# Softmax sums by another transfer queue, and weight copies off GpSimd

## The chip, the cores and the metric

The kernel runs on one core of a Trainium2 chip. The core has TensorE (matrix products), VectorE, ScalarE, GpSimd and SyncE (SP), each with an instruction queue of its own, and 16 engines for transfers. Time is that of the device for one execution, in microseconds (us); lower is better. In the rows, PE is TensorE's products, PEld its weight loads, DVE is VectorE, ACT ScalarE, POOL GpSimd, and SPq the queue of SP that issues transfers.

## What is computed

An attention over a window with sinks, and two feed-forward layers behind it. Shapes: 2 batches, 8 heads, 768 positions, head width 64; 4 sinks, window 128; 1536 tokens, model width 512, inner width 2048.

```python
scores = q @ k.T / 8                      # kept: the 4 sinks, and the last 128 positions up to the row
a = exp(scores - max); a = a / (sum(a) + 1e-9)
x = a @ v                                 # heads side by side: 1536 x 512
h = x @ w_in                              # first layer: a rational function
g = (a0 + a1*h + a2*h**2 + a3*h**3) / (1 + abs(b0)*abs(h) + abs(b1)*h**2 + 1e-6)
x = g @ w_out
h = x @ moe2_w_in                         # second layer: h * sigmoid(1.702 h)
out = (h * sigmoid(1.702*h)) @ moe2_w_out
```

The weights arrive as 64-bit floats and are turned into 32-bit ones on the chip.

## The kernel before

**Tiling.** The 1536 tokens are three blocks T of 512 (TB). The attention of a block works on pairs of heads, four pairs for each block, so there are twelve rounds. The feed-forward layers take the 2048 inner columns in 16 slices f of 128; a unit is a block with half of the slices, and UNITS gives their order, so that a weight slice serves several blocks before it is dropped. Each product of two 32-bit matrices is three TensorE products of a high and a low part (wh with xh, wh with xl, wl with xh).

**A weight slice** (decode, L629): SP loads it to wraw; ScalarE takes an absolute value (dy), VectorE clamps and shifts and joins (dy, dt); then `hi(WH, ...)` at L641 copies dt to the high part of wi or wo, on one of the engines that WH names, and VectorE subtracts that for the low part. There are 64 slices, and 64 copies of that kind.

**A round of the attention.** TensorE multiplies q and k; VectorE masks and finds the maximum (m, nm); ScalarE exponentiates (a) and sums (sm). sums (L978) adds 1e-9, takes the reciprocal (rs), has TensorE transpose the eight columns to eight rows, and copies them to rt (ScalarE or VectorE). One transfer writes rt to DRAM (rd); two transfers read it back to rb, each spreading four rows over 64 partitions (the two heads). Meanwhile TensorE transposes a, ScalarE or VectorE copies that to th and sT, and values (L1031) multiplies with v. VectorE multiplies that with rb, ScalarE rounds to xh, VectorE makes xl: the input of the first layer.

**The first layer's function** (el_a, L725). ScalarE makes y = |b0 h| and z from the square, and GpSimd issues a transfer that adds y to z in place (add, L544). ScalarE's logarithm and exponential then make the reciprocal r (el_b).

**The order.** Nothing is issued in the order of the program text. A planner (play, L292) simulates the five engines with a price for each operation and a due time: the longest path to the end plus BIAS of its class (at0 to at2: the attention of a block; wi00, wo01 and so on: the slices of layer and half; m0 to m7: the units). HEAD spaces the rounds of a block in that due time. An engine that becomes free takes its own most urgent ready operation, and, where it has none, one of another engine that has a form for it, if `spares` allows it:

```python
return max(free[p], now) + q + o.alts[p][0] > now + o.alts[e][0] + THETA   # L393
```

The first engine named in "act/dve/pool" is the owner p, the others may take over (e). What the planner wrote down is then the fixed order of each queue. Where TensorE has nothing ready in the first part, it gets filler products on zeros (L869). The transfers are planned with L234 to L237. A queue issues in order: an instruction that waits holds what stands behind it.

Of the kernel before, what the change touches and what calls it, by code (L numbers as in the profile page):

```python
# [6 lines left out]
F32R = mybir.dt.float32r  # L7
# [7 lines left out]
B, H, S, D = 2, 8, 768, 64  # L15
# [30 lines left out]
PSUM_TAGS, ANY_ORDER = ("h", "acc", "att"), ("att", "m")  # L46

GH2, GL2 = "act", "dve"
WH, WL, XH, S2, ST = "act/dve/pool", "dve", "act", "pool/dve", "act/dve"
TH, PE_OUT = "act/dve", "act/dve"  # L50

BIAS = {
# [4 lines left out]
}  # L57
HEAD = (5.81, 0.28, 18.6, 1.92)
THETA = -1.79

WARM, FILL, FILL_AHEAD = 20, 6000, 0.1

# [11 lines left out]
ADD_FIX, ADD_LAT = 0.9, 1.6  # L74
# [70 lines left out]
def overlap(a, b):  # L145
    return all(x[0] < y[1] and y[0] < x[1] for x, y in zip(a, b))


class Program:
# [56 lines left out]
    def op(self, eng, meth, alloc=(), alts=(), given=False, calls=(), cost=0.0, **kw):  # L206


        o = Op()
        o.i, o.eng, o.own = len(self.ops), eng, eng  # L210
        o.cat = self.cat
        o.table = 2 if kw.get("func") == AF.Sigmoid else 1 if kw.get("func") in (AF.Exp, AF.Ln) else 0
        views = [(k, v) for c in calls or [kw] for k, v in c.items() if isinstance(v, View)]

        def runner(eng, meth, kw):
            def run():
                a = {k: v.real() if isinstance(v, View) else v for k, v in kw.items()}
                e = getattr(self.nc, eng)
                if meth in ("matmul", "memset"):
                    return getattr(e, meth)(a.pop("out"), **a)  # L220
                return getattr(e, meth)(**a)  # L221
            return run
        o.lat = LAT
        o.nbytes = o.columns = 0
        if calls:
            runs = [runner(eng, meth, c) for c in calls]
            o.alts = {eng: (cost, lambda: [f() for f in runs][-1])}
            o.cost, o.lat = cost, PE_LAT
            o.columns = sum(c["rhs"].n * 4 * (c["lhsT"].box[0][1] - c["lhsT"].box[0][0]) / P if "rhs" in c else 2 * P for c in calls)
        elif meth == "dma_start":  # L230
            v = views[0][1]
            o.nbytes = (v.box[0][1] - v.box[0][0]) * v.n * 4
            o.cost, o.lat = 0.45 if v.box[0][1] - v.box[0][0] == P else 0.62, DMA_LAT
            if eng == "gpsimd":  # L234
                o.nbytes *= 2
                o.cost, o.lat = ADD_FIX, ADD_LAT + 0.6 * (kw["out"].dtype == F32R)
            o.alts = {eng: (o.cost, runner(eng, meth, kw))}  # L237
        else:
            self.columns = 0
            o.alts = {e: (self.price(e, m_, k_), runner(e, m_, k_)) for e, m_, k_ in [(eng, meth, kw)] + list(alts)}  # L240
            o.cost = min(c for c, _ in o.alts.values())
            o.columns = self.columns
            if eng == "tensor":
                o.lat = PE_LAT
        if given:
            o.alts, o.cost, o.lat, o.nbytes = {eng: (1e-6, lambda: None)}, 1e-6, given * 1.25 - 0.75, 0
        pre = {}
        for k, v in views:
            w = k in ("out", "accum_out")
            for q, box, wr in v.t.acc:  # L250
                if (w or wr) and overlap(box, v.box):
                    pre[q.i] = q
            if not v.t.acc:
                assert w, (v.t.name, k)
        o.allocs = [v.t for k, v in views if not v.t.acc] + [v.t for v in alloc if not v.t.acc]
        o.allocs = list(dict.fromkeys(o.allocs))
        o.begun = []
        for t in o.allocs:
            t.first = o
            t.acc.append((o, ((0, 0),), False))  # L260
        for t in dict.fromkeys([v.t for _, v in views] + [v.t for v in alloc]):
            if t not in o.allocs and not any(v.t is t for _, v in views):
                t.acc.append((o, ((0, 0),), False))
            if t.first is not o and t.first.i not in pre and (t.first.i, 0) not in pre:
                t.first.begun.append(o)
                pre[t.first.i, 0] = None
        for k, v in views:
            v.t.acc.append((o, v.box, k in ("out", "accum_out")))
        o.tiles = list(dict.fromkeys([v.t for _, v in views] + [v.t for v in alloc]))
        o.banks = [t for t in o.tiles if t.tag in PSUM_TAGS]  # L270
        o.preds = len(pre)
        o.succ = []
        o.next = []
        for q in pre.values():
            if q is not None:
                q.succ.append(o)
        o.ready = 0.0
        self.ops.append(o)
        return o
# [12 lines left out]
    def play(self):  # L292
# [92 lines left out]
        def spares(o, e):  # L385
# [3 lines left out]
            for t, i in own[p]:  # L389
                if t >= -o.prio:  # L390
                    break
                q += ops[i].alts[p][0]
            return max(free[p], now) + q + o.alts[p][0] > now + o.alts[e][0] + THETA  # L393

# [112 lines left out]
def emit(tc, qT, kX, vL, w_in, w_out, ca, cb, nw, out):  # L507
    nc = tc.nc
    R = Program(nc, tc)
# [12 lines left out]
    def hi(eng, o, i):  # L522
        l = eng.split("/")
        return one_of([form(e, o, i) for e in l])
# [3 lines left out]
    def tt(eng, op, out, in0, in1):  # L528
        return one_of([(NAMES[e], "tensor_tensor", dict(out=out, in0=in0, in1=in1, op=op)) for e in eng.split("/")])
# [322 lines left out]
    def build_banded():  # L852
        with (
# [23 lines left out]
            def attention(T, xs, alone):  # L877
# [49 lines left out]
                def pst(kind):  # L927
                    if alone and kind == "s":
                        return R.tile(ps, [P, 512], F32, tag="acc", name="pss", bufs=4)
                    if alone and kind == "v":  # L930
                        return R.tile(ps, [P, 512], F32, tag="h", name="psv", bufs=H_BUFS)
                    return R.tile(ps, [P, 512], F32, tag="att", name="psa", bufs=8 - 4 - H_BUFS)
# [45 lines left out]
                def sums(h):  # L978

                    sm = st.pop(("sm", h))  # L980
                    assert nq == 4
                    rs = R.tile(ap, [P, 8], F32, tag="rs", name="rs", bufs=2)
                    R.op("vector", "tensor_scalar", out=rs, in0=sm, scalar1=EPS_SM, scalar2=None, op0=ALU.add)
                    R.op("vector", "reciprocal", out=rs, in_=rs)
                    p = pst("t")
                    R.op("tensor", "transpose", out=p[:8, :P], in_=rs, identity=ident)
                    rt = R.tile(ap, [8, P], F32, tag="rt", name="rt", bufs=2)
                    hi(ST, rt, p[:8, :P])
                    rd = R.tile(dp, [8, P], F32, tag="rd", name="rd", bufs=4)
                    R.op("sync", "dma_start", out=rd, in_=rt)  # L990
                    rb = R.tile(ap, [P, 4 * P], F32, tag="rb", name="rb", bufs=2)
                    for e in (0, 1):
                        R.op("sync", "dma_start", out=rb[e * D:(e + 1) * D], in_=rd[4 * e:4 * e + 4].spread(D))
                    st["rb", h] = rb

                def sinks(h):
# [61 lines left out]
                def first_of(h):  # L1058
# [3 lines left out]
                    if h:  # L1062
                        R.follow(firsts[-2], firsts[-1], 2 * HEAD[T])

                for r in range(-1, H // 2 + 1):
                    if 0 <= r < H // 2:
                        items.append(lambda h=2 * r: first_of(h))
                    if 0 <= r - 1:
                        items.append(lambda h=2 * r - 2: (sums(h), sinks(h) if sq else 0, transposes(h), transposes(h + 1), values(h)))
                    if 0 <= r + 1 < H // 2:  # L1070
                        items.append(lambda h=2 * r + 2: (load(h), load(h + 1)))
# [144 lines left out]
```

## Time and profile before

| | us |
|---|---|
| median of 3 runs (lowest to highest) | 675.73 (673.58 to 675.84) |
| the profiled execution, its time | 675.01 |
| its span, first to last instruction | 673.0 |

| engine | busy us | share of the span |
|---|---|---|
| TensorE | 652.1 | 97% |
| VectorE | 502.3 | 75% |
| ScalarE | 373.3 | 55% |
| GpSimd | 66.8 | 10% |

A busy share is a mean over stages with different limits, so the stages are read one by one. Their edges, read from the kinds of TensorE's products: the attention of the first block to about 70 us, that of the others beside the first products to 160 us, the first layer to about 400 us, the second layer to 660 us, and the last sums and stores.

### The profile page before, as it was taken

What the parts mean: (1) busy time and instruction counts of PE and PEld (TensorE: products, weight loads), DVE (VectorE), ACT (ScalarE), POOL (GpSimd) and SP (SyncE); (2) the same over time, 40 slices, a digit from 0 to 9 for tenths busy, and PEclk for the clock granted to TensorE, in tenths of its full rate; (3) what the DMA queues carried; (4) which work ended last, traced back from release to release, by engine and by line L of the source; (5) the groups of instructions that cost most, each with busy time, mean ns of one, the idle gap of its engine ahead of it and who ended that gap; (6) DMA issues with size and microseconds to landing.
All of it is one profiled execution on the core that took longest, in us unless ns stands there. A gap on an engine that the chain in (4) does not pass through costs nothing.

```text
span 673.0 us, 8941 instructions
## 1 busy us (share of the span) xinstructions
PE 652.1 (97%) x3128; PEld 499.3 (74%) x3128; DVE 502.3 (75%) x1019; ACT 373.3 (55%) x734; POOL 66.8 (10%) x86
## 2 busy tenths in 40 slices
PE   7999999999999999999998999999999999999995
PEld 5666666557887777778887877877887777787874
DVE  5999989985959999999998999972788522312241
ACT  4877879785857685677856754442344222222130
POOL 1101101001214121111121100000000000000000
PEclk7999999999999999999999999999999999999999
DMA  5767675731424353554441424440233100010011
GB/s 169 231 192 214 178 209 162 202 88 47 86 43 84 72 141 78 110 134 86 110 109 32 94 71 140 134 126 0 67 121 94 31 1 0 1 63 0 17 47 67
DMA packets 31972, 64.87 MB, mean 96 GB/s; under 512 B 6224, under 2 KB 12464, under 8 KB 31920
## 3 DMA queue, kind: packets, MB, share of 16 engines
q1 hardware_dynamic: 24720, 51.64, 24.8%
q0 software_dynamic: 6912, 12.59, 11.2%
q8 instruction: 26, 0.43, 0.3%
q14 instruction: 26, 0.21, 0.1%
q10 hardware_dynamic: 288, 0.00, 0.0%
HBM read 48.44 MB, written 3.19 MB: 77 GB/s over the span
## 4 chain that ended last, share of the span: by engine, by line
PE 73%; DVE 11%; DMA 6%; issue 5%; ACT 3%; POOL 1%; SPq 0%; DVEq 0%; POOLq 0%; ACTq 0%
PE att L220 26%; PE acc L220 24%; PE h L220 18%; DMA z<-y 4%; PE att L221 4%; DVE s L221 3%; DVE dt L221 3%; PE acc L869 1%; DVE z L221 1%; DMA q<-q_t 1%; ACT r L221 1%; DVE gh L221 1%; DVE gl L221 1%; DMA wraw<-w_out 1%; DVE wo L221 1%
## 5 line engine op out<-in xcount | busy, mean ns | idle before, releaser
L220 PE MATMUL h<-xh,wi 128*128 128x512 f32 x416 | 142.7, 397 | 0.5 <-POOL wi L221 0.3
L220 PE MATMUL att<-xh,wi 128*128 128x512 f32 x352 | 116.6, 392 | 0.3 <-DVE y L221 0.3
L220 PE MATMUL acc<-gh,wo 128*128 128x512 f32 x272 | 93.5, 399 | 1.6 <-DVE gh L221 1.6
L220 PEld LDWEIGHTS h<-xh,wi 128*128 128x128 f32 x416 | 77.9, 188 | 19.6 <-issue 1.8
L221 DVE TENSOR_TENSOR gl<-y,gh 128x512 fp32r<-128x512 f32 x48 | 34.3, 718 | 77.2 <-ACT gh L221 45.4
L220 PE MATMUL acc<-wo,gh 128*128 128x512 f32 x288 | 91.4, 396 | 0.2
L221 DVE SCALAR_TENSOR_TENSOR dt<-wraw,dt 128x512 int32<-128x512 int32 x128 | 86.8, 687 | 1.2
L221 ACT ACTIVATE gh<-y 128x512 fp32r<-128x512 f32 x48 | 30.3, 632 | 96.9 <-PE acc L220 81.2
L220 PE MATMUL h<-xl,wi 128*128 128x512 f32 x208 | 82.1, 395 | 0.0
L220 PEld LDWEIGHTS att<-xh,wi 128*128 128x128 f32 x352 | 66.1, 188 | 16.1 <-DVE y L221 1.1
L220 PE MATMUL att<-xl,wi 128*128 128x512 f32 x176 | 68.8, 391 | 0.0
L221 POOL DMA_DIRECT2D z<-y x48 | 42.2, 880 | 248.1 <-ACT z L221 222.4
L220 PEld LDWEIGHTS acc<-wo,gh 128*128 128x128 f32 x288 | 53.3, 188 | 14.0 <-ACT gh L221 2.1
L220 PEld LDWEIGHTS acc<-gh,wo 128*128 128x128 f32 x272 | 50.5, 188 | 14.1 <-issue 1.8
L221 ACT ACTIVATE dy<-wraw 128x512 f32<-128x512 f32 x64 | 42.6, 666 | 26.8 <-DMA wraw<-w_in 16.6
L220 PE MATMUL acc<-gl,wo 128*128 128x512 f32 x136 | 52.7, 403 | 1.6 <-DVE gl L221 1.5
L221 ACT ACTIVATE r<-z,ln_b 128x512 f32<-128x512 f32 x48 | 34.8, 724 | 31.8 <-DMA z<-y 31.7
L221 ACT ACTIVATE a<-m,nm 128x272 f32<-128x272 f32 (+1 forms) x96 | 47.1, 492 | 9.0 <-DVE nm L221 8.3
L220 PE MATMUL acc<-wo,gl 128*128 128x512 f32 x144 | 49.6, 394 | 0.0
L220 PEld LDWEIGHTS h<-xl,wi 128*128 128x128 f32 x208 | 39.1, 188 | 9.7 <-issue 1.5
L221 DVE SCALAR_TENSOR_TENSOR gh<-s,a_t,r 128x512 fp32r<-128x512 f32 x48 | 36.1, 755 | 9.9 <-PE acc L220 5.9
L220 PE MATMUL att<-gh,wo 128*128 128x512 f32 x112 | 40.2, 394 | 1.8 <-ACT xh L221 1.8
(123 smaller groups left out, 1120.8 us busy)
## 6 DMA issues: line engine op xcount, KB each, us to landing
wraw<-w_in SPq DMA_DIRECT2D x32, 512.0 KB, 3.7
wraw<-w_out SPq DMA_DIRECT2D x32, 512.0 KB, 3.6
z<-y POOLq DMA_DIRECT2D x48, 256.0 KB, 3.3
rb<-rd SPq DMA_DIRECT2D x24, 128.0 KB, 4.6
vr<-v_l SPq DMA_DIRECT2D x16, 160.0 KB, 4.7
q<-q_t SPq DMA_DIRECT2D x8, 256.0 KB, 4.6
out<-xf SPq DMA_DIRECT2D x8, 256.0 KB, 2.5
k<-k_x SPq DMA_DIRECT2D x4, 360.0 KB, 4.0
```

What stands on the lines that cost most here:

```text
L220: return getattr(e, meth)(a.pop("out"), **a)
L221: return getattr(e, meth)(**a)
L869: nc.tensor.matmul(R.real[k][:, 0:256], lhsT=zero[:, :P], rhs=zero, start=True, stop=True)
```

## The change

The copies at L641 may go to ScalarE or VectorE, no longer to GpSimd. The three transfers of a round (L990, L993) are issued by GpSimd instead of SP. The planner's price of a GpSimd transfer counts double bytes only for adds. BIAS, HEAD and THETA get other values, so that all queues are ordered anew.

```diff
-WH, WL, XH, S2, ST = "act/dve/pool", "dve", "act", "pool/dve", "act/dve"
+WH, WL, XH, S2, ST = "act/dve", "dve", "act", "pool/dve", "act/dve"
 BIAS = {
-    "at0": 30.94, "at1": 72.58, "at2": 21.27, "at3": -64.03, "m0": -7.08, "m1": 59.83, "m2": 7.83,
-    "m3": -6.08, "m4": 58.6, "m5": -74.99, "m6": -3.71, "m7": 80.95, "sb": -38.42, "wi00": 11.26,
-    "wi01": 4.06, "wi10": -52.4, "wi11": -0.71, "wo00": -183.01, "wo01": 66.68, "wo10": -33.34,
-    "wo11": -3.14,
+    "at0": 88.77, "at1": 34.81, "at2": 33.63, "at3": -156.21, "m0": -23.44, "m1": 34.02, "m2": 32.74,
+    "m3": -76.69, "m4": 57.28, "m5": -44.67, "m6": -22.11, "m7": 53.1, "sb": -182.86, "wi00": -31.63,
+    "wi01": 25.46, "wi10": -95.8, "wi11": -11.59, "wo00": -155.25, "wo01": 46.56, "wo10": -126.52,
+    "wo11": -78.91,
 }
-HEAD = (5.81, 0.28, 18.6, 1.92)
-THETA = -1.79
+HEAD = (4.59, 16.33, 17.07, 6.27)
+THETA = 0.21
...
             if eng == "gpsimd":
-                o.nbytes *= 2
-                o.cost, o.lat = ADD_FIX, ADD_LAT + 0.6 * (kw["out"].dtype == F32R)
+                if "accum_op" in kw:
+                    o.nbytes *= 2
+                o.cost, o.lat = ADD_FIX, ADD_LAT
...
-                    R.op("sync", "dma_start", out=rd, in_=rt)
+                    R.op("gpsimd", "dma_start", out=rd, in_=rt)
                     rb = R.tile(ap, [P, 4 * P], F32, tag="rb", name="rb", bufs=2)
                     for e in (0, 1):
-                        R.op("sync", "dma_start", out=rb[e * D:(e + 1) * D], in_=rd[4 * e:4 * e + 4].spread(D))
+                        R.op("gpsimd", "dma_start", out=rb[e * D:(e + 1) * D], in_=rd[4 * e:4 * e + 4].spread(D))
```

## Rows read from the trace of the kernel before

**Rows 1.** Busy time of each engine by stage, then granted clock, transfers' share, GB/s.

```profile
6.00:70.00 64.00, 59.99 (x409) 40.21 (x409) 55.67 (x182) 49.33 (x148) 6.75 (x10) 0.95 0.72 215
70.00:160.00 90.00, 88.36 (x559) 56.86 (x559) 79.18 (x216) 70.00 (x182) 8.02 (x10) 1.00 0.55 154
160.00:400.00 240.00, 234.70 (x1012) 188.56 (x1011) 224.66 (x370) 168.62 (x263) 45.40 (x51) 1.00 0.41 89
400.00:660.00 260.00, 259.58 (x1114) 205.72 (x1113) 138.04 (x235) 84.08 (x142) 5.31 (x6) 1.00 0.17 55
660.00:673.00 13.00, 5.23 (x23) 3.94 (x21) 2.48 (x4) 0.00 (x0) 0.00 (x0) 0.89 0.24 86
```

**Rows 2.** The same view of the filler's line L869 alone, first stage (PE, PEld).

```profile
6.00:70.00 64.00, 16.18 (x88) 12.60 (x88) 0.95 0.72 215
```

**Rows 3.** Waits, 160 to 400 us: who waited for whom, total us, times, longest.

```profile
PEld acc L220 <- DVE gl L221: 3.1, 4, 1.2
```

**Rows 4.** Operations by tile (dt, th): count, ns shortest/median/longest, first and last start.

```profile
L221 POOL TENSOR_SCALAR wi<-dt x14: 610/730/2418, 17.3 to 348.1; 128x512 fp32r<-128x512 f32 x14
L221 ACT ACTIVATE wi<-dt x14: 618/634/635, 46.0 to 512.5; 128x512 fp32r<-128x512 f32 x14
L221 POOL TENSOR_SCALAR wo<-dt x13: 613/752/1521, 41.0 to 580.4; 128x512 fp32r<-128x512 f32 x13
L221 DVE CAST wi<-dt x4: 421/424/427, 162.0 to 497.5; 128x512 fp32r<-128x512 f32 x4
...
L221 DVE COPY th<-att x10: 546/684/692, 21.7 to 154.8; 128x512 f32<-128x512 f32 x6, 128x384 f32<-128x384 f32 x4
```

**Rows 5.** GpSimd's timeline (start, us, what): first and last copy before 400 us.

```profile
17.32 0.62 POOL L221 TENSOR_SCALAR wi<-dt 128x512 fp32r<-128x512 f32 x1 [10.35 <-DVE dt L221]
...
348.06 0.61 POOL L221 TENSOR_SCALAR wi<-dt 128x512 fp32r<-128x512 f32 x1 [0.51 <-PE att L220]
```

**Rows 6.** VectorE: the shift by tile (as rows 4), and two stretched operations, timeline.

```profile
L221 DVE TENSOR_SCALAR dt<-dy x64: 414/422/1436, 12.5 to 525.9; 128x512 int32<-128x512 int32 x64
...
17.46 0.76 DVE L221 TENSOR_SCALAR dt<-dy 128x512 int32<-128x512 int32 x1
...
348.18 1.03 DVE L221 TENSOR_TENSOR wi<-dt,wi 128x512 fp32r<-128x512 f32 x1
```

**Rows 7.** Waits of ScalarE between 20 and 160 us.

```profile
ACT dy L221 <- DMA wraw<-w_in: 3.9, 4, 2.1
```

**Rows 8.** Timeline of the first and last round: SP's issues, VectorE's product with rb.

```profile
21.58 0.35 SPq L221 DMA_DIRECT2D rd<-rt  x1
25.73 1.14 SPq L221 DMA_DIRECT2D rb<-rd  x2
30.71 0.69 DVE L221 TENSOR_TENSOR rb<-h,rb 128x512 f32<-128x512 f32 x1 [0.95 <-DMA rb<-rd]
...
152.40 0.28 SPq L221 DMA_DIRECT2D rd<-rt  x1
153.69 1.09 SPq L221 DMA_DIRECT2D rb<-rd  x2
159.84 0.69 DVE L221 TENSOR_TENSOR rb<-att,rb 128x512 f32<-128x512 f32 x1 [4.40 <-PE att L220]
```

**Rows 9.** VectorE's waits for rb, and rb's transfers from issue to landing.

```profile
DVE rb L221 <- DMA rb<-rd: 2.9, 4, 1.0
...
DMA to landing us min/median/max: 3.2/4.6/5.3
```

**Rows 10.** Tile z, 60 to 160 us: GpSimd's adding transfers, issue (ns) and landing.

```profile
L221 POOL DMA_DIRECT2D z<-y x7: 865/888/1067, 63.0 to 143.4; - x7
DMA to landing us min/median/max: 3.3/4.1/6.2
```

**Rows 11.** Waits between 60 and 160 us, of GpSimd and of ScalarE.

```profile
POOL z L221 <- ACT z L221: 52.5, 6, 11.4
...
ACT r L221 <- DMA z<-y: 3.2, 2, 2.6
```

## The prediction

> **What bounds the kernel now.** I read the busy time by stage first, because an average over the span would hide that its stages have different limits. [rows 1] cuts the span into five: the first block's attention (6 to 70 us), the rest of the attention beside the first matrix products (70 to 160), the rational stage (160 to 400), the sigmoid stage (400 to 660) and the tail. TensorE is idle for 4.0, 1.6, 5.3, 0.4 and 7.8 us in them (length less busy time), at a granted clock of 1.00 from 70 to 660 us. So from 70 us on TensorE sets the end, and an edit there can win back only the 6.9 us of 70 to 400. Before 70 us it is different: 16.2 us of TensorE's busy time there are the filler's 88 products on zeros [rows 2], which run only where nothing real is ready.
>
> Who makes TensorE wait? VectorE is busy 87%, 88% and 94% of the first three stages and 53% of the fourth; ScalarE 77%, 78%, 70% and 32% [rows 1]. In 160 to 400 us the longest wait of TensorE's weight loads ends with VectorE (gl, 3.1 us) [rows 3]. So VectorE's time before 400 us is what an edit can turn into a gain, at best as far as TensorE idles or runs the filler; after 400 us almost everything is covered.
>
> The profiled execution took 675.01 us for a span of 673.0, so 2.0 lie around it. The median of the runs, 675.73, is 0.1% above. I make the sum against 675.0.
>
> **Part 1: GpSimd takes no weight copies.** GpSimd makes 14 + 13 = 27 of the 64 copies t to wh; one on ScalarE takes 0.634 us, on VectorE 0.424 [rows 4]. 21 of the 27 start before 400 us (7 before 70, 4 by 160, 10 by 400), the first at 17.32, the last at 348.06 [rows 5].
>
> What goes away: while such a copy runs, VectorE operations stretch. 12 stretched ones stand before 400 us, from a shift of 0.76 us (median 0.422, longest 1.436) to a subtraction of 1.03 [rows 6]; their excess over the median of their form adds up to 4.6 us. Stretching works the other way too: one GpSimd copy took 2.418 us, median 0.730 [rows 4]. VectorE gets at most 4.6 us back; I take -2, since TensorE idles in only a part of the places. Bounds -4.6 and 0.
>
> What comes in its place: 21 copies. All on ScalarE they are 21 x 0.634 = 13.3 us beside 288 us of work in 394, which fits, price 0. All on VectorE they are 21 x 0.424 = 8.9 us on the engine that is late. ScalarE is the first choice in the code and idles more, so I put three quarters there and 5 copies on VectorE: +2. Bounds 0 and +8.9. If ScalarE's cover were gone (6 to 160 us, where it is at 77 to 78%), its 11 copies there would cost 7.0 us. The six copies after 400 us cost nothing: VectorE is at 53%.
>
> **Part 2: THETA from -1.79 to 0.21.** A second engine now takes work only if it ends at least 0.21 us sooner; before, it could end 1.79 us later. VectorE made 10 of the th copies at 0.546 to 0.692 us, 6.3 us in all and all before 160 us [rows 4]. I let half go back to ScalarE: -3. Bounds -6.3 and 0.
>
> **Part 3: the rows of one over the sums go through GpSimd's queue.** Twelve rounds of three transfers, 36 issues, leave SP. What follows on SP is the loads of k, q, v and weights. ScalarE waits for w_in only 3.9 us between 20 and 160 us [rows 7] and is not the latest engine, so I price that at nothing; bounds -3.9 and 0. On GpSimd an accumulate issued between 60 and 150 us takes 0.89 us [rows 10]; 36 x 0.89 = 32 us, on an engine that is busy 14.8 of the 154 us up to 160 [rows 1]. Its own time is hidden.
>
> What counts is the latency of a round and the adds (z from y) queued behind it. On SP the first round took 21.58 to 30.71 = 9.1 us from rd's issue to the product that waited 0.95 us for it, because other loads stood ahead of rb until 25.73; the last, with little queued, issued rb 1.29 us after rd and landed some 6.4 us after it (1.29 + 0.55 for the second issue + 4.6) [rows 8, 9]. For GpSimd no row shows such a round; the nearest is the accumulate, which lands 3.3 to 6.2 us after its issue, median 4.1 [rows 10]. Lower end: rd as quick as on SP, 1.3 + 0.9 + 3.3 = 5.5 us. Upper end: 3.3 + 0.9 + 6.2 = 10.4. I take 3.3 + 0.9 + 4.1 = 8.3, nearer to the accumulate than to SP's rd: 0.8 better than a queued SP round, 1.9 worse than a free one. VectorE waited for rows four times, 2.9 us in all [rows 9]; those waits mostly go, while the last round would land near 160.7 instead of before 159.84, where the product waited for TensorE's values, not for the rows [rows 8]: +0.9. Together -2 on VectorE, of which I take -1. Bounds -2.9 and +4 (another four rounds with a wait of 1.0).
>
> A rule of the Trainium skill speaks against this part. The rows: in the stage where VectorE is at 88% the accumulates' issue took 0.865 to 1.067 us, so at most 0.2 us were lost to anything VectorE did [rows 10]. The page "SBUF — State Buffer", section "SBUF: two separate sides", warns that transfers issued from GpSimd need descriptors written by it, that VectorE's two-port operations lock it out meanwhile, and gives about 620 ns alone against 3100 ns overlapped. By that page's ratio the 36 issues would take 36 x 2.5 = 90 us more of GpSimd, an estimate; by the row 36 x 0.2 = 7, hidden. The trace so far does not bear the larger figure out.
>
> **Part 4: BIAS and HEAD.** They put every queue in another order. The trace has no row for an order that did not run. Its scale is what TensorE loses now: an equally good order gives 0, a perfect one from 70 to 400 us -6.9, one twice as bad +6.9 [rows 1]. I take 0: the planner's rule is the same, and no row says which way the new numbers err.
>
> **Sum.** -2 + 2 - 3 - 1 + 0 = -4, so 675.0 - 4 = 671.0 us.
>
> **The rivals.** *Hidden (about 675).* The relief is on VectorE, and TensorE is busy 97.8% of 160 to 400 us. If the places where VectorE comes free are not those where TensorE waits, only a quarter of the -4 shows. For: most of the stretched operations have TensorE busy beside them. Against: the filler before 70 us shows VectorE and ScalarE pacing there.
>
> *Slower (about 683).* GpSimd's queue keeps its order. A round now holds it from rd's issue through rd's landing to the second rb: 0.89 + 3.3 + 2 x 0.89 = 6.0 us; eight rounds after 60 us hold it 48 of 100 us. GpSimd issues 7 adds there; 3.4 would fall into a round and wait 3.0 us on average, 10 us in all, while ScalarE's logarithm and all that is queued behind it waits. ScalarE idles 20 of 90 us between 70 and 160 [rows 1], which absorbs perhaps 2: +8. For: ScalarE already waits 3.2 us for them there [rows 11]. Against: GpSimd waits for ScalarE before those adds, 52.5 us in six waits [rows 11], so there are large gaps, and the planner places an add that is ready between rd and rb. It decides when ScalarE's wait for z between 60 and 160 us grows from 3 to above some 10 us. The lock-out rule above would act in the same place, by making the round longer, and has its chance in this one.
>
> *Much faster (about 660).* The new weights in BIAS raise the first block's attention from 19.7 above its weights' preparation (30.94 - 11.26) to 120 (88.77 + 31.63). If that ends the attention sooner, a good half of the 16.2 us of filler becomes useful time, -11 on top of the sum. Against: the earlier order already let the attention through first in most places, and what is put off has to be done by an engine at 94% later.
>
> **How the numbers follow.** Forecast 0.45 (about 662 to 672), hidden 0.28, slower 0.21, much faster 0.06. A measurement of this kernel can tell about 0.5%, 3.4 us, from no change. Faster by more than that: 0.45 + 0.06 = 0.51; within it 0.28; slower 0.21. Without the order the unknown costs reach from -17.7 (all lower ends) to +12.9 (all upper ends), which hardly fall together; for 8 in 10 I leave out most of the much faster case and the worse half of the slower one: 662 to 682.
>
> **What the changed profile would show.** Right: no GpSimd copy of weights and no shift on VectorE near 1.4 us; fewer th copies on VectorE; rows landing 6 to 9 us after rd's issue with VectorE waiting under 3 us for them; fewer than 88 filler products or less idle time in 160 to 400. Wrong: ScalarE waiting over 10 us for z before 160 us; VectorE waiting several us for rows; the same busy times with TensorE's idle time moved from one stage to another, which would make the order, not the edits, the cause. Most of all the unpriced new order can make this wrong.

## The result, and the profile of the changed kernel

The changed kernel takes 681.36 us (median of 11 runs, 675.66 to 684.34) beside 675.73 us for the kernel before (11 runs, 673.58 to 677.93). The ratio is 1.007, with a 95% interval of 1.0049 to 1.009: slower by some 5 us, where 671.0 was forecast. The profiled execution took 680.79 us. Of all executions in this document one, at 690.49 us, is left out as slow (the first kernel of the last table).

The head of the page of the changed kernel: span, busy time of each engine, and TensorE's granted clock in 40 slices of 17 us, in tenths.

```profile
span 678.9 us, 8855 instructions
...
PE 654.0 (96%) x3107; PEld 500.6 (74%) x3107; DVE 498.7 (73%) x1025; ACT 380.9 (56%) x755; POOL 66.1 (10%) x95
...
PEclk7999999997999999999999999999999999999998
```

Busy time by stage, changed kernel (the columns of [rows 1]: the stretch and its length, busy us of PE, PEld, DVE, ACT and POOL with their instructions in brackets, granted clock, transfers' share, GB/s):

```profile
6.00:70.00 64.00, 58.48 (x393) 39.07 (x393) 52.03 (x177) 50.40 (x150) 10.00 (x18) 0.95 0.69 204
70.00:160.00 90.00, 84.30 (x506) 53.67 (x505) 76.73 (x213) 71.03 (x185) 16.12 (x24) 0.97 0.59 158
160.00:400.00 240.00, 235.22 (x1023) 186.57 (x1023) 219.29 (x368) 167.43 (x266) 38.50 (x44) 1.00 0.40 86
400.00:660.00 260.00, 259.91 (x1120) 207.95 (x1119) 144.16 (x248) 90.12 (x154) 0.00 (x0) 1.00 0.19 59
```

Set against [rows 1], the loss stands in one stage, 70 to 160 us. TensorE's idle time there rose from 1.6 to 5.7 us, and the granted clock fell from 1.00 to 0.97, which over 90 us is up to another 2.7 (a part of it falls into the idle time itself). In the clock line the second 7 is the tenth slice, 153 to 170 us: there the clock was lost. The other stages moved little: 160 to 400 us idles 4.8 us instead of 5.3, 400 to 660 us 0.1 instead of 0.4. VectorE, the late engine, is *less* busy up to 400 us than before (52.0, 76.7, 219.3 us against 55.7, 79.2, 224.7), and the kernel became slower all the same. Little of that is relief: over the span VectorE is busy 498.7 us instead of 502.3, and 6.1 us more of it than before stand in 400 to 660 us.

What VectorE waited for at the product of the rows (whole span: total us, times, longest):

```profile
DVE rb L221 <- DMA rb<-rd: 17.8, 11, 4.3
```

That was 2.9 us in four waits [rows 9]. Now 11 of the 12 rounds wait. The longest one, round 11, in the timeline (start, us, engine, what, in brackets the idle time before it and what ended that):

```profile
146.60 0.54 POOL L221 DMA_DIRECT2D rd<-rt  x1 [2.25 <-ACT rt L221]
...
150.60 1.15 POOL L221 DMA_DIRECT2D rb<-rd  x2 [3.46 <-DVE dt L221]
...
151.02 0.42 DVE L221 TENSOR_SCALAR dy<-dy 128x512 f32<-128x512 f32 x1
...
153.63 0.73 PE L220 MATMUL h<-xh,wi 128*128 128x512 f32 x2
155.74 0.69 DVE L221 TENSOR_TENSOR rb<-att,rb 128x512 f32<-128x512 f32 x1 [4.30 <-DMA rb<-rd]
156.47 0.63 ACT L221 ACTIVATE xh<-rb 128x512 fp32r<-128x512 f32 x1 [4.57 <-DVE rb L221]
...
156.49 2.18 PE L221 MATMUL att<-ident,a 128*128 128x128 f32 x9 [2.13 <-DVE rb L221]
...
158.32 0.78 PE L220 MATMUL h<-xl,wi 128*128 128x512 f32 x1
```

Read it from top to bottom. rd leaves at 146.60, the two rb at 150.60 (rb reads what rd writes, so it needs rd's landing, whatever releaser the bracket names last), and they land at about 155.7. VectorE has ended its previous operation at 151.44 and stands for 4.30 us; ScalarE stands behind it for 4.57 and TensorE for 2.13. Then look at the matmuls' durations: two products of 128x512 took 0.73 us before the gap, and after it one takes 0.78.

The same place in slices of 1 us (columns as in the stages; the clock is the third figure from the end):

```profile
154.00:155.00 1.00, 0.36 (x2) 0.00 (x0) 0.00 (x0) 0.00 (x0) 0.00 (x0) 1.00 0.23 49
155.00:156.00 1.00, 0.00 (x0) 0.00 (x0) 0.26 (x1) 0.00 (x0) 0.00 (x0) 0.52 0.00 0
...
160.00:161.00 1.00, 1.00 (x4) 0.77 (x4) 0.56 (x4) 0.75 (x2) 0.00 (x0) 0.50 0.00 0
161.00:162.00 1.00, 1.00 (x7) 0.54 (x5) 0.00 (x0) 0.52 (x1) 0.00 (x0) 0.56 0.00 0
162.00:163.00 1.00, 1.00 (x11) 0.93 (x9) 0.00 (x0) 0.87 (x4) 0.13 (x1) 1.00 0.00 0
```

TensorE has nothing to do from 154.36, the granted clock is at 0.50 (1.2 GHz) from about 155, and it is back at 1.00 (2.4 GHz) only near 162, after 5 us of uninterrupted work. Work of 156.49 to 161.9 at half speed is some 2.7 us lost; with the 2.1 us of idle time this one wait is worth an estimated 4.8 us, worked out from these rows.

This is one execution, and not every execution lost as much clock. Of the 11, the three with a mean granted clock of 0.991 to 0.993 took 675.66, 677.77 and 679.64 us; the eight with 0.981 to 0.987, the profiled one among them, took 680.79 to 684.34. The means are 4.7 us apart. That agrees with the estimate, though where the others lost their clock was not recorded.

### The profile page after: what moved, and what is told of

It reads as the page before. It is cut to its first block, busy times and chain, and to the rows that moved or that the text cites. A ratio compares the mean times of both kernels' runs of the same rounds, so it can differ in the third digit from the quotient of the medians.

```text
span 678.9 us, 8855 instructions
## 1 busy us (share of the span) xinstructions
PE 654.0 (96%) x3107; PEld 500.6 (74%) x3107; DVE 498.7 (73%) x1025; ACT 380.9 (56%) x755; POOL 66.1 (10%) x95
## 3 DMA queue, kind: packets, MB, share of 16 engines
q0 software_dynamic: 8448, 15.78, 12.7%
## 4 chain that ended last, share of the span: by engine, by line
PE 54%; issue 23%; DMA 9%; DVE 6%; POOL 5%; ACT 3%; SPq 0%; POOLq 0%; DVEq 0%
PE att L220 23%; PE acc L220 16%; PE h L220 13%; DMA rb<-rd 4%; POOL z L221 4%; DMA rd<-rt 2%; PE att L221 2%; DVE dt L221 1%; DVE m L221 1%; DVE s L221 1%; DMA q<-q_t 1%; DMA z<-y 1%; DMA wraw<-w_out 1%; POOL rb L221 1%; PE acc L870 1%
## 5 line engine op out<-in xcount | busy, mean ns | idle before, releaser
L220 PE MATMUL att<-xh,wi 128*128 128x512 f32 x352 | 118.1, 392 | 0.4 <-DVE s L221 0.4
L220 PE MATMUL acc<-gh,wo 128*128 128x512 f32 x272 | 95.3, 400 | 1.6 <-DVE gh L221 1.6
L221 DVE TENSOR_TENSOR gl<-y,gh 128x512 fp32r<-128x512 f32 x48 | 32.8, 690 | 74.6 <-ACT gh L221 45.5
L220 PE MATMUL acc<-wo,gh 128*128 128x512 f32 x224 | 78.7, 395 | 0.0
L221 POOL DMA_DIRECT2D z<-y x48 | 43.7, 916 | 210.7 <-ACT z L221 205.7
L220 PE MATMUL att<-wo,gh 128*128 128x512 f32 x160 | 61.1, 400 | 0.1
L220 PE MATMUL acc<-gl,wo 128*128 128x512 f32 x136 | 54.1, 405 | 1.4 <-DVE gl L221 1.4
L221 ACT ACTIVATE a<-m,nm 128x272 f32<-128x272 f32 (+1 forms) x96 | 47.0, 491 | 11.3 <-DVE nm L221 11.0
L220 PEld LDWEIGHTS acc<-wo,gh 128*128 128x128 f32 x224 | 41.6, 188 | 10.5 <-ACT gh L221 1.8
L221 PE MATMUL att<-ident,a 128*128 128x128 f32 (+1 forms) x240 | 38.7, 289 | 5.1 <-DVE rb L221 4.2
```

## The experiments

Two kinds have to be kept apart. In the first, the order of the instructions on TensorE, VectorE and ScalarE is that of the named kernel: the planner still prices what it priced, and only the last step, which emits the instruction, names another engine. In the second the planner orders everything anew. Each run is compared with the kernel before on the same chip (medians there 675.44, 675.13 and 675.20). Medians of different chips are set beside each other below; where it matters, the difference of the two ratios to before is given too.

**Rows back on SP, in the changed kernel's order.**

```diff
-            o.alts = {eng: (o.cost, runner(eng, meth, kw))}
+            o.alts = {eng: (o.cost, runner("sync" if views[0][1].t.name in ("rd", "rb") else eng, meth, kw))}
```

> The changed kernel with its order on TensorE, VectorE and ScalarE kept instruction for instruction; only the 36 row transfers are issued by SP instead of GpSimd, at the place in time that the plan gave them. Theory R (the rows land too late for the places that the new order gives to the products with them): on SP rd lands in 1.3 to 2 us instead of 3.5, VectorE's wait for rows falls from 17.8 us to under 8, the granted clock stays at 1.00 between 150 and 165 us, the time falls to 675 to 678 us. Theory O (the new order as such is worse, whoever carries the rows): within 680 to 683 us, the clock dip at 155 to 162 us stays.

Measured: 673.67 us (671.0 to 677.76), 0.9974 of before [0.9955, 0.9993]. VectorE's wait for rows in this kernel:

```profile
DVE rb L221 <- DMA rb<-rd: 5.2, 4, 1.8
```

Its second stage, and the stretch around round 11 by the same columns:

```profile
70.00:160.00 90.00, 88.56 (x554) 57.57 (x554) 80.31 (x217) 73.87 (x191) 6.06 (x7) 1.00 0.57 161
...
155.00:160.00 5.00, 5.00 (x34) 3.02 (x33) 4.47 (x7) 1.12 (x2) 0.88 (x1) 1.00 0.47 108
```

The landing of its rb after the issue:

```profile
DMA to landing us min/median/max: 2.7/3.0/4.1
```

With nothing but the queue of 36 transfers undone, 7.7 us come back (by the two ratios to before, 0.0096 of 675, 6.5 us), the wait for rows falls from 17.8 to 5.2 us, TensorE's idle time in the second stage from 5.7 to 1.4, and the clock stays at 1.00. The rows' move is the cause of the slowdown; what remains of the change is 1.8 us faster than before, and faster than the 675 to 678 us that theory R expected.

**Rows on GpSimd, in the order of before.** The same line of the kernel before, with "gpsimd" for "sync".

> The kernel before with its order kept; only the 36 row transfers are issued by GpSimd instead of SP. Theory R: rows later by up to 2 us in rounds that SP served without a queue, about the same in the others; VectorE's wait for rows from 2.9 us to 5 to 10, the time up by 1 to 4 us, 677 to 680. Theory O: the queue matters little, wait for rows under 5 us, time 675 to 677 us.

Measured: 677.44 us (675.34 to 679.54), 1.0027 [1.0013, 1.0041]; VectorE waits 5.0 us for rows, in five waits. The same move costs only 2.0 us here. The transfers cost time in both orders; how much differs, and the place that the order gives to the product is the reason argued for below. In this order the waits for rows did not go either: they rose from 2.9 to 5.0 us.

**The 27 GpSimd copies made by ScalarE, in the order of before.** Where the planner chose GpSimd, the emitted copy is ScalarE's:

```diff
-            o.alts = {e: (self.price(e, m_, k_), runner(e, m_, k_)) for e, m_, k_ in ...}
+            o.alts = {e: (self.price(e, m_, k_), runner(*(("scalar", "activation", dict(out=k_["out"], in_=k_["in0"], func=AF.Copy)) if e == "gpsimd" else (e, m_, k_)))) for e, m_, k_ in ...}
```

> The kernel before with its order kept; only the 27 weight copies of GpSimd are made by ScalarE, at the place in time that the plan gave them. The prediction's part 1: the stretching of VectorE (4.6 us before 400 us) goes away, ScalarE gets 17 us more work beside idle time: 673 to 676 us. Rival: ScalarE, at 77 to 78 percent before 160 us, passes 11 x 0.63 us on: 677 to 681 us.

Measured: 674.03 us (672.73 to 676.75), 0.9982 [0.997, 0.9995], 1.4 us faster. VectorE's shifts in this kernel (count, ns shortest/median/longest):

```profile
L221 DVE TENSOR_SCALAR dt<-dy x64: 412/420/441, 11.7 to 524.8; 128x512 int32<-128x512 int32 x64
```

The longest of 64 is now 0.441 us where it was 1.436 [rows 6]. The stretching came from GpSimd's copies, and taking them away is worth a little by itself.

**One leg at a time, in the changed kernel's order.** First rd alone on SP, then rb alone (the emitter's condition names one tile).

> The changed kernel, its order kept; only the first leg of a round (rd, 12 transfers) is issued by SP, the second (rb, 24) stays with GpSimd. Theory A (the first leg's latency on GpSimd is what makes rows late): VectorE's wait for rows falls from 17.8 us to under 9, time 674 to 677 us. Theory B (the second leg, or what stands between the legs on GpSimd's queue, makes them late): wait 13 us or more, time 678 to 682 us.

> The mirror image: the changed kernel, its order kept; rd stays with GpSimd, only rb (24 transfers) is issued by SP. Theory A: wait 12 us or more, time 678 to 682 us. Theory B: wait under 9 us, time 674 to 677 us.

| on GpSimd | VectorE waits for rows, us (times) | median us (range) | ratio to before |
|---|---|---|---|
| neither | 5.2 (4) | 673.67 (671.0 to 677.76) | 0.9974 [0.9955, 0.9993] |
| rd | 9.3 (8) | 675.30 (673.99 to 680.62) | 1.0007 [0.9987, 1.0026] |
| rb | 12.7 (7) | 676.72 (673.18 to 679.47) | 1.0012 [0.999, 1.0034] |
| both | 17.8 (11) | 681.36 (675.66 to 684.34) | 1.007 [1.0049, 1.009] |

Neither theory held, and neither leg is the whole of it. Each adds some microseconds of waiting, rb more than rd, and in these four kernels the time rises with the wait: 12.6 us more waiting, 7.7 us more time. Going from one leg to two costs more (6.1 or 4.6 us) than the first leg did (1.6 or 3.1). That would come out if slack in the order is used up first, which no run shows directly. It would also come out of the clock: in the second stage TensorE was granted 1.00 with rd alone on GpSimd, 0.98 with rb alone and 0.97 with both.

**Round 11 alone.** One run puts only round 11 on SP, another leaves only round 11 on GpSimd; both keep the changed kernel's order.

```diff
+... runner("sync" if views[0][1].t.name in ("rd", "rb") and len(self.order["rd"]) == 11 else eng, meth, kw) ...
+... runner("sync" if views[0][1].t.name in ("rd", "rb") and len(self.order["rd"]) != 11 else eng, meth, kw) ...
```

> The changed kernel, its order kept; only the three transfers of round 11, whose product waited 4.3 us and after which TensorE idled 2.1 us and ran 155 to 162 us at the lower clock, are issued by SP; 33 transfers stay with GpSimd. Theory C (most of the loss is that one idle stretch and the clock behind it): no granted clock below 1.00 between 150 and 165 us, 675 to 678 us. Theory D (the loss is the sum of eleven waits, some 0.7 us each): 680 to 682 us.

> The changed kernel, its order kept; the rows of eleven rounds go through SP, only those of round 11 through GpSimd: the complement of the run in which round 11 alone went through SP. Theory C (that round's idle stretch and the clock behind it carry most of the loss by themselves): TensorE idles about 2 us near 150 us, the clock dips, 676 to 679 us. Theory D (lateness of one round is taken up if the others are in time): 673 to 675 us, no dip.

Only round 11 on SP: 677.12 us (672.57 to 680.93), 1.0018 [0.9994, 1.0041], 4.2 us under the changed kernel. Its clock is at 1.00 from 150 to 165 us, but VectorE's wait for rows is still 17.8 us, so other rounds wait instead: in its profile round 3 waits 4.7 us, TensorE stands for 5.1 us up to 49.05, and the clock is at 0.50 there until near 53 us. The lost clock was moved to the first stage, where theory C had not looked. Only round 11 on GpSimd: 675.57 us (674.09 to 678.71), 1.0012 [0.9994, 1.003], 1.9 us above the run without it (2.6 by the two ratios), between the two theories; the wait for rows is 8.2 us, 4.2 of them in round 11, before which TensorE stands for 2.08. Its windows:

```profile
150.00:155.00 5.00, 3.88 (x15) 3.44 (x16) 3.11 (x10) 2.96 (x8) 0.00 (x0) 0.50 0.00 0
155.00:160.00 5.00, 5.00 (x30) 3.57 (x30) 1.36 (x4) 4.13 (x8) 0.28 (x1) 0.84 0.01 4
```

One late round is enough to bring the clock to 0.50 and to cost 1.9 us; with the others late as well, making it punctual gives back 4.2. It is a part of the 7.7 us and not the whole. Time is not a matter of the summed wait alone: the changed kernel and the run with only round 11 on SP both wait 17.8 us for rows in their profiles.

**The planner told better prices for the rows.** The changed kernel plans a GpSimd row transfer at the price of an add without bytes doubled; here it is given a shorter issue (0.55 us instead of 0.9) and a later landing (3.0 us behind the bytes instead of 1.6), and orders everything anew.

```diff
-                o.cost, o.lat = ADD_FIX, ADD_LAT
+                o.cost, o.lat = (ADD_FIX, ADD_LAT) if "accum_op" in kw else (0.55, 3.0)
```

> The changed kernel, planned anew with another price of a row transfer on GpSimd: 0.55 us of issue and 3.0 us behind its bytes, as the trace of the changed kernel shows (0.53 to 0.55; rd 3.5 us and rb 4.0 us from issue to landing), instead of 0.9 and 1.6. The whole order changes with it. Theory R: products with rows get later places, VectorE's wait for rows falls below 8 us, no clock dip before 170 us, 673 to 678 us. Theory O: 679 to 683 us, whatever the wait for rows.

Measured: 680.22 us (677.89 to 686.13), 1.01 [1.0066, 1.0135]. The wait for rows fell to 3.4 us and TensorE's idle time in the second stage to 1.2, as theory R had it, and against theory R next to nothing was won. (The profile is of the fastest of the six executions, 677.89 us.) TensorE's longest waits in this kernel (total us, times, longest):

```profile
PE att L220 <- DVE wi L221: 3.5, 2, 3.3
PE att L220 <- DVE th L221: 3.1, 1, 3.1
```

The order is another, and loses time in other places: TensorE idles 5.9 us from 160 to 400 us, and 3.5 from 400 to 660, where [rows 1] had 0.4.

**Other orders.** Four more kernels were planned anew. The changed kernel with "sync" in its three calls; the kernel before without GpSimd in WH; the kernel before with THETA 0.21; and the changed kernel with BIAS, HEAD and THETA of before.

```diff
-                    R.op("gpsimd", "dma_start", out=rd, in_=rt)
+                    R.op("sync", "dma_start", out=rd, in_=rt)
...
-WH, WL, XH, S2, ST = "act/dve/pool", "dve", "act", "pool/dve", "act/dve"
+WH, WL, XH, S2, ST = "act/dve", "dve", "act", "pool/dve", "act/dve"
...
-THETA = -1.79
+THETA = 0.21
```

> The changed kernel with the rows given back to SP in the plan too, so that the whole order is made anew with the new BIAS, HEAD and THETA and without GpSimd copies. If a good order goes with these numbers: 672 to 675 us, near the 673.7 of the kept order with rows on SP. If these numbers fit only the order they came with: 676 to 684 us, as with the newly priced plan (680.2).

> The kernel before with one edit of the change alone, WH without GpSimd, planned anew with its own BIAS, HEAD and THETA; rows on SP. In the kept order taking the copies from GpSimd gave 674.0 us. If the plan follows the prices faithfully: 672 to 676 us. If any new plan lands some us higher, as two new plans of the changed kernel did (680.2 and 684.6): 678 to 686 us.

> The kernel before with THETA 0.21 alone, planned anew. The prediction's part 2: fewer th copies on VectorE, 3 us less: 671 to 674 us. If a new plan as such costs more than the edit gives: 678 to 686 us.

> The changed kernel with BIAS, HEAD and THETA of before, planned anew: rows on GpSimd, copies off GpSimd. If the change's new numbers are what makes its order bad: 674 to 678 us. If numbers and program belong together, and any other pairing is worse: 680 to 690 us.

| planned anew | wait for rows, us | median us (range) | ratio to before |
|---|---|---|---|
| rows on SP, new numbers | 2.4 | 684.26 (679.79 to 688.37) | 1.0131 [1.009, 1.0171] |
| rows on SP, old numbers, no GpSimd copies | 1.0 | 670.18 (668.13 to 674.17) | 0.9933 [0.9911, 0.9955] |
| before with THETA 0.21 | 2.4 | 675.10 (673.0 to 678.27) | 1.0 [0.9979, 1.0021] |
| changed kernel, old numbers | 11.3 | 681.02 (680.49 to 682.79) | 1.0093 [1.0062, 1.0124] |

Of the expectations only the last was met, in its second range; the first kernel came out just above its second range, the second below both, the third between both. The second is faster than both kernels: part 1 of the change alone, 5.0 us under before. In the kept order the same part gave 1.4; the rest is the new order's. The fourth differs from the second in the rows' queue and the planner's price for GpSimd transfers, with the same numbers: 10.8 us. Its first stages:

```profile
6.00:70.00 64.00, 58.88 (x397) 39.31 (x397) 53.99 (x183) 46.84 (x143) 9.32 (x17) 0.92 0.65 203
70.00:160.00 90.00, 83.81 (x496) 53.14 (x494) 76.66 (x212) 68.86 (x180) 15.68 (x25) 0.96 0.57 155
```

The picture is that of the changed kernel: in the second stage TensorE idles 6.2 us and the clock is at 0.96. So the slowdown does not need the new numbers. How much of the 10.8 us is the rows' and how much the new order's is not shown, since both are orders made anew. The first of the table shows that an order can be bad without any wait for rows. From 250 to 350 us it ran so:

```profile
250.00:300.00 50.00, 45.36 (x183) 35.91 (x182) 48.75 (x86) 33.70 (x53) 6.94 (x8) 0.93 0.46 114
300.00:350.00 50.00, 45.88 (x189) 35.98 (x188) 44.64 (x77) 33.39 (x53) 6.40 (x8) 0.97 0.39 85
```

TensorE idles 8.8 of these 100 us; the changed kernel idles 4.8 in the 240 us of that whole stage. Why that order is bad was not settled, nor was that of the priced one; no run takes such an order apart. What the two show is the scatter: a small change of a price or a name moves all queues, and these orders lie up to 14 us apart.

## Why the prediction was wrong, point by point

**What bounds the kernel**: held. TensorE sets the end, VectorE makes it wait before 400 us, and the loss of the change came through VectorE. Missing was the clock. The prediction read the granted clock of 1.00 in [rows 1] as a fact of those stages; in the changed kernel, with a gap of 2.13 us, the second stage shows 0.97. So TensorE's idle time was priced at its own length, where this gap cost an estimated 4.8.

**Part 1, the copies** (0 net, between -4.6 and +8.9): right that they stretch VectorE's operations, and better than its net of 0. In the order of before, with all 27 copies on ScalarE, their removal gives -1.4 us (0.9982); with a new order around it -5.0 (0.9933). Where the copies went in the changed kernel it had wrong. VectorE made 9 in the kernel before, the 4 of wi in [rows 4] and these of wo:

```profile
L221 DVE CAST wo<-dt x5: 426/427/428, 62.5 to 529.8; 128x512 fp32r<-128x512 f32 x5
```

The changed kernel's shifts and weight copies by tile:

```profile
L221 DVE TENSOR_SCALAR dt<-dy x64: 409/424/505, 12.5 to 532.1; 128x512 int32<-128x512 int32 x64
...
L221 ACT ACTIVATE wo<-dt x23: 612/630/663, 43.1 to 588.0; 128x512 fp32r<-128x512 f32 x23
L221 ACT ACTIVATE wi<-dt x20: 612/632/657, 19.5 to 518.7; 128x512 fp32r<-128x512 f32 x20
...
L221 DVE CAST wi<-dt x12: 404/422/430, 22.4 to 504.7; 128x512 fp32r<-128x512 f32 x12
L221 DVE CAST wo<-dt x9: 375/426/428, 95.2 to 586.3; 128x512 fp32r<-128x512 f32 x9
```

VectorE makes 21, and 15 of them before 400 us instead of 4: 11 more where the prediction put 5, some 4.6 us of VectorE's time instead of 2. What they cost by themselves no run shows; with the rows on SP the kernel is faster than before in spite of them. And of its copies of th, those that VectorE makes:

```profile
L221 DVE COPY th<-att x4: 683/689/692, 21.8 to 159.3; 128x512 f32<-128x512 f32 x4
```

No shift above 0.505 us is left, as foretold.

**Part 2, THETA** (-3): the mechanism was there and the gain was not. VectorE makes 4 copies of th instead of 10 [rows 4]. The kernel before with this THETA alone makes 7 there, and at 1.0 [0.9979, 1.0021] it is where it was. A gain of 3 us (0.44%) is outside that interval.

**Part 3, the rows** (-1, between -2.9 and +4): the step that failed. The latency was sized well: 8.3 us from rd's issue to the landing was taken, and over the twelve rounds the product of the changed kernel starts 7.5 to 10.5 us after rd's issue, 8.6 on average. What was wrong is the sentence that follows it, "those waits mostly go". They rose from 2.9 to 17.8 us. The sentence sets a round by GpSimd beside a queued round by SP, the first one, and leaves the product where it was. But a wait is the landing less the product's place in VectorE's order. Eight of the twelve rounds of before had their rows in time, and lose that margin when the rows come later; and the new order moved the place. Worked out from the timelines of the twelve rounds (start of the product, less its wait, less the end of rt): on average 8.5 us after rt in the kernel before and 7.5 in the changed one, in its last two rounds 5.1 and 5.5. With 0.3 us from rt to rd's issue and 8.6 to the landing, the rows come 8.9 us after rt: 1.4 us late on average, and about 4 in round 11. In the order of before, where the product stands later, the waits rise only to 5.0 us and the move costs 2.0 us, inside the bounds and of the other sign; in the changed order 7.7, outside them. That the place makes the difference between 2.0 and 7.7 is argued from these timelines; no run moves the place alone. The clock that TensorE lost behind round 11, an estimated 2.7 us, had no term in the sum at all. The upper bound of +4 took "another four rounds with a wait of 1.0"; it was another seven, of 1.6 on average over all eleven.

**Part 4, the order** (0): right for the order by itself. With the rows on SP, the changed order (673.67) is as good as that of before without GpSimd's copies (674.03). But part 4 was priced apart from part 3, and it is the order that decides whether part 3's latency is waited for.

**The rivals.** *Slower (683)* came nearest to the time by luck: its mechanism did not happen. It had the rows' round hold up the adds of z, and ScalarE's wait for z grow above 10 us. ScalarE's waits from 60 to 160 us:

```profile
ACT xh L221 <- DVE rb L221: 9.5, 5, 4.6
ACT r L221 <- DMA z<-y: 4.0, 3, 2.5
...
ACT dy L221 <- DMA wraw<-w_in: 0.3, 1, 0.3
```

The wait for z went from 3.2 [rows 11] to 4.0 us; what ScalarE waits for is VectorE's product. Nor was it the other way round. In six of the twelve rounds an add of some 0.94 us stood between rd and rb, but it did not hold rb up: by the timelines rb follows rd after 2.2 to 4.5 us in these six and after 3.4 to 4.4 in the other six. SP's relief is there and won no time that shows: ScalarE's wait for w_in in this stretch fell from 2.9 to 0.3 us. *Much faster (660)*: the filler's line from 6 to 70 us reads

```profile
6.00:70.00 64.00, 13.26 (x63) 9.67 (x62) 0.95 0.69 204
```

so without the filler TensorE did 45.2 us of real work there instead of 43.8 [rows 1, 2]: 1.4 us of the 11 that this rival put in. *Hidden (675)* is out too: the changed kernel is slower by more than 0.49%.

**GpSimd's time.** The page "SBUF — State Buffer" of the Trainium skill, section "SBUF: two separate sides", named GpSimd's transfers as the danger, and the danger was real, but not where the prediction put the page's figure, into the time of an issue. The rows' issues on GpSimd in the changed kernel, by tile:

```profile
L221 POOL DMA_DIRECT2D rb<-rd x24: 521/554/914, 25.0 to 166.2; - x24
L221 POOL DMA_DIRECT2D rd<-rt x12: 523/532/777, 21.6 to 162.9; - x12
```

The issues of the adds from 60 to 160 us:

```profile
L221 POOL DMA_DIRECT2D z<-y x7: 931/943/1169, 64.1 to 143.4; - x7
```

An issue took 0.53 to 0.55 us in the middle and at most 0.914, beside a VectorE that is busy 85% in the second stage. So no issue of a row took more than 1.7 times its median. That page of the Trainium skill gives its 620 and 3100 ns for a whole transfer, alone and beside a VectorE copy. Whether the longer landings by GpSimd hold such a lock-out no run here separates: none changes what VectorE does beside them. The cost came from when the rows landed and from the product's place, not from GpSimd's busy time.

**The signs named ahead.** "VectorE waiting several us for rows" stood among those that would show the forecast wrong, and it is what the first view of the changed kernel shows. It had no price among the rivals.

## What to carry to other kernels

A transfer's latency costs what it exceeds the consumer's place in its engine's order, so price both in the order that will run; a re-planned order may have moved the consumer, and then a right latency gives a wrong sum. Where a planner reorders everything, undo one part at the last step, the emission, with the order kept: that separated 7.7 us of cause from orders that scatter between 670 and 684 us. And when the engine that sets the end gets a gap, look at its granted clock behind the gap before pricing it.

## What the runs showed of the hardware

- In the changed kernel TensorE was idle for 2.13 us from 154.36. Its granted clock fell to 0.50 (1.2 GHz) within that gap, near 155, and stayed there until near 162 us, through some 5 us of uninterrupted work. The run with only round 11 on GpSimd shows the same in a gap of 2.08 us. A product of 128x512 took 0.78 us there; over the whole span that form takes 0.40 on average.
- Not every gap is followed by that. A gap of 1.35 us that ended at 71.78 in the changed kernel left the clock at 1.00; one of the same 1.35 us that ended at 75.10 in the changed kernel with the old numbers had 0.50 behind it from 76 to 82 us.
- rb, 128 KB, landed in a median of 3.0 us when SP issued it and of 4.0 us when GpSimd did, both in the changed kernel's order. In the order of before it was 4.6 us by either queue, so the queue alone does not set it. The changed kernel's row, beside the one of rows on SP above:

```profile
DMA to landing us min/median/max: 2.8/4.0/6.2
```

- From the end of rt to rd's issue a median of 0.3 us passes on GpSimd (changed kernel) and of 0.03 on SP (kernel before).
- A GpSimd copy of weights stretched VectorE's shift from 0.42 to 1.44 us [rows 6]; without such copies no shift took over 0.51.
